# Linear attention and feed-forward on one core: a searched order of operations for the first token group, zero matmuls for TensorE's clock, and the first key chunk on ScalarE's DMA queue

## The chip, the cores and the metric

The kernel runs on one core of one Trainium2 chip. The metric is device time in microseconds (us), the median over executions. Engines are named as in the profile: PE is TensorE's matmuls, PEld its weight loads, DVE is VectorE, ACT is ScalarE, POOL is GpSimd, SP is SyncE, which issues 134 of the 135 DMAs in the kernel before.

## The reference, cut to what matters

```python
q, k, v: (4, 8, 768, 64) float32      # batch, heads, sequence, head width
w_in: (512, 2048), w_out: (2048, 512)

for b in range(12):                   # blocks of 64 positions; the kernel uses 128
    intra = einsum('bhic,bhjc->bhij', qb, kb) * Dmask      # lam ** (i-j), causal
    intra = einsum('bhij,bhjd->bhid', intra, vb)
    inter = einsum('bhid,bhde->bhie', qb * lam_pow, kv_state)
    out[:, :, sl] = intra + inter
    kv_state = lam_block * kv_state + einsum('bhsd,bhse->bhde', kb_dec, vb)
x = out.transpose(0, 2, 1, 3).reshape(3072, 512)
h = x @ w_in
return (h * sigmoid(h)) @ w_out
```

## The kernel before

The 3072 tokens are 24 chunks of 128, and eight token groups of 256 to 512 tokens. For each chunk the kernel scales queries and keys by powers of lam ("pq", "pk"), transposes them on TensorE ("tq", "tk"), copies the transposes to SBUF ("qt", "kt"), computes scores ("s"), masks them ("m"), forms the output ("o") and the running state ("d", "kv"). A group then goes through the up-projection (16 blocks of hidden features, m=0 to 15, through w_in) and the down-projection (through w_out). Weights arrive as float32 and are cast to bf16 on chip ("w"): w_in in five chunks (0 and 1 are the two halves of the rows for m=0..3; chunk 2 is for m=4..7, chunk 3 for m=8..11, chunk 4 for m=12..15), w_out in four.

The order of the first group stands in a string; each word is one operation with its chunk. Every engine's instructions are written in that order, and the trace keeps it: TensorE's work for tq:0, tk:0, d:0, s:0,0, tk:1 and s:0,1 starts at 8.46, 9.46, 9.85, 10.57, 10.97 and 11.40 us.

```python
ORDER = """
pq:0,1 pq:0,0 pk:0 tq:0 vc:0 qt:0 tk:0 d:0 pk:1 qt:1 kt:0,0 kt:0,1 s:0,0 kv:0 tk:1 m:0,0 s:0,1 pq:2,1
... (two lines cut)
vc:3 f:0 w:1 o:3 x:2 xa:3 xb:3 d:3 f:1 kv:3 g:0
"""
    def prep_q1(c, r):                       # half of a pair of query chunks, on GpSimd
        ...
        nc.gpsimd.tensor_tensor(qpairs[c][:, r, :, :], rawq[c][:, :, r, :],
                                lam_fwd[:, NB + c % NB + r, :][:, :, None].to_broadcast([128, H, D]), op=AL.mult)
    # loads, all on SyncE's queue, in this order:
    load_q(0), load_k(0), load_v(0), load_k(1), load_q(2), load_v(1)
    load_k(2), load_k(3), load_v(2), load_v(3)
    for i in range(4):
        load_w("in", i)
    load_q(4)                                # queries of chunks 4 and 5
    load_k(4), load_v(4)
    load_w("in", 4)
    load_k(5), load_v(5)
    load_w("out", 0)
    # after ORDER: m=0..3 of group 0 are done
    cast_w("in", 2)
    ...
    for m in range(4, 8): ffn1(0, m)
    for m in range(8, 11): ffn1(0, m)
    vcast(4)
    tq4 = pe_tq(4, "att", 3); copy_qt(4, tq4), copy_qt(5, tq4)
    tk4 = pe_tk(4, "att", 3)
    copy_kt(4, tk4, 0, nc.vector), copy_kt(4, tk4, 1, nc.vector)
    cast_w("in", 4)                          # on VectorE
    ffn1(0, 11)
    ...
    st_s(4), st_d(4)                         # scores and masks of chunk 4, its state
    ffn1(0, 12)                              # first use of w_in chunk 4
    st_o(4)
    ...
    cast_w("out", 0)
```

## Time and profile before

| | before |
|---|---|
| median of 3 runs | 226.31 us (225.83 to 226.37) |
| profiled run | 226.1 us, span 224.4 us |
| first matmul | 8.46 us |
| m=4 of group 0 starts | 25.94 us |
| w_in chunk 4 has landed | 33.59 us |

All times below are counted from the start of the span. First the page of the kernel before, busy tenths of 40 slices of 5.6 us each, for TensorE, its granted clock and the DMA engines:

```profile
PE   0488998899999999999999999999999999999993
...
PEclk9999999999999999999999999999999999999999
DMA  4999999999959999999999998897420110110212
```

Only the first eight slices of TensorE (45 us) are partly below 9; after them it is full to the end. The DMA row is at 9 in nearly every slice from the second to the 27th: the 16 DMA engines are busy nearly all of that time. The clock row must be read with care. It shows 9 from the start, but the first clock record of this trace, full clock, is at 17.3 us, and until then matmuls issue only every 107 ns (below). What the clock was before that has to be read from the matmuls.

The chain of waits that ended last, by engine:

```profile
PE 82%; DVE 7%; ACT 4%; issue 2%; DMA 2%; POOL 1%
```

Then lines of TensorE's timeline (start, duration, engine, line, output<-inputs, shapes, count; in brackets the idle time before it and what ended it):

```profile
8.46 1.03 PE L271 MATMUL tq<-ident,qb_180 128*128 128x128 bf16 x8 [8.46 <-POOL qb_180 L219]
...
16.83 0.62 PE L285 MATMUL tk<-ident,kb 128*128 128x128 bf16 x4
17.25 0.42 PE L315 MATMUL kv_ps<-vpad_103,kb 128*128 128x128 bf16 x4
...
23.32 8.83 PE L383 MATMUL h_ps<-xt,w_in_bf 128*128 128x256 bf16 x51
...
35.27 0.81 PE L383 MATMUL h_ps<-xt,w_in_bf 128*128 128x512 bf16 x3 [0.60 <-DVE w_in_bf L165]
...
40.39 1.19 PE L398 MATMUL o_ps<-w_out_bf,g 128*128 128x512 bf16 x4 [0.32 <-DVE w_out_bf L167]
```

The first matmul waits for GpSimd's scaled queries. Four matmuls of 128 columns show 0.62 us in one line and 0.42 us in the next: near 17.3 us, where the record of full clock begins, they became almost twice as fast. From the starts of such groups that is one matmul per 107 ns before and 56 ns after. At 35.27 us TensorE waits for VectorE's cast of w_in chunk 4, at 40.39 us for that of w_out chunk 0.

The same stretch on VectorE:

```profile
26.91 1.23 DVE L165 CAST w_in_bf<-w_tmp 128x2048 bf16<-128x2048 f32 x1 [1.64 <-DMA w_tmp<-in_moe_w_in_dram]
...
33.76 1.23 DVE L165 CAST w_in_bf<-w_tmp 128x2048 bf16<-128x2048 f32 x1
35.02 1.29 DVE L341 TENSOR_TENSOR ss<-sp,mask 128x512 bf16<-128x512 f32 x2
```

The cast at 26.91 us (w_in chunk 3) waited 1.64 us for its DMA. The cast at 33.76 us (chunk 4) shows no wait, but the chunk had landed only at 33.59 us, 0.17 us earlier: it had no slack either. The masks of chunk 4 stand behind that cast. Who TensorE waited for between 20 and 45 us (total, times, longest):

```profile
PE h_ps L383 <- DVE w_in_bf L165: 0.6, 1, 0.6
PE o_ps L398 <- DVE w_out_bf L167: 0.3, 1, 0.3
```

### The profile page before, as it was taken

The numbers are of one execution on the slowest core, as the hardware profiler recorded it, in microseconds if no ns is written. First come the engines' busy times: TensorE is split into PE (matmuls) and PEld (weight loads), VectorE is DVE, ScalarE is ACT, GpSimd is POOL, SyncE is SP. The second block draws the span as 40 slices with busy tenths as digits, with TensorE's granted clock in tenths as the row PEclk, the third lists the DMA queues.
The fourth block names the chain that finished last, engine by engine and source line by source line (L and its number), as shares of the span: only waits on it lengthen the run. The fifth ranks groups of instructions, "written<-read, shape, count | busy, mean of one in ns | idle before, by whom it ended". The sixth has DMA issues, their size and how long they took to land.

```text
span 224.4 us, 3867 instructions
## 1 busy us (share of the span) xinstructions
PE 206.6 (92%) x1496; PEld 126.5 (56%) x1520; DVE 93.7 (42%) x181; ACT 100.6 (45%) x199; POOL 51.5 (23%) x58
## 2 busy tenths in 40 slices
PE   0488998899999999999999999999999999999993
PEld 0376755566455786666556656655666644444441
DVE  6468516742168772353443613551454310011121
ACT  4858676444202576455345345444545344433000
POOL 2770051025513222423333330333000000000000
PEclk9999999999999999999999999999999999999999
DMA  4999999999959999999999998897420110110212
GB/s 124 241 223 383 312 269 338 376 235 233 262 148 211 162 217 164 212 203 148 225 211 179 188 248 112 167 203 165 122 67 3 47 50 0 48 47 0 96 47 93
DMA packets 97027, 38.02 MB, mean 169 GB/s; under 512 B 86768, under 2 KB 89840, under 8 KB 97008
## 3 DMA queue, kind: packets, MB, share of 16 engines
q1 hardware_dynamic: 96864, 37.76, 77.8%
q8 instruction: 12, 0.20, 0.4%
q14 instruction: 7, 0.06, 0.1%
q10 hardware_dynamic: 144, 0.00, 0.0%
HBM read 27.27 MB, written 6.29 MB: 150 GB/s over the span
## 4 chain that ended last, share of the span: by engine, by line
PE 82%; DVE 7%; ACT 4%; issue 2%; DMA 2%; POOL 1%
PE h_ps L383 35%; PE o_ps L398 35%; PE op L362 6%; PE sp L336 4%; DVE ss L341 3%; DMA lam_sb<-in_lam_dram 2%; PE kv_ps L315 1%; PE tq L271 1%; DVE ob L402 1%; POOL qb_180 L219 1%; ACT L121 1%; DVE ktbd_104 L262 1%; DVE w_in_bf L165 1%; ACT qt L277 0%; PE tk L285 0%
## 5 line engine op out<-in xcount | busy, mean ns | idle before, releaser
L383 PE MATMUL h_ps<-xt,w_in_bf 128*128 128x384 bf16 (+2 forms) x524 | 98.0, 321 | 1.1 <-DVE w_in_bf L165 0.6
L387 ACT ACTIVATE g<-h_ps 128x384 bf16<-128x384 f32 (+2 forms) x128 | 62.5, 491 | 74.7 <-PE h_ps L383 72.5
L398 PE MATMUL o_ps<-w_out_bf,g 128*128 128x512 bf16 x364 | 91.8, 379 | 1.4 <-DVE w_out_bf L167 0.3
L383 PEld LDWEIGHTS <-w_in_bf 128*128 128x128 bf16 x528 | 50.0, 98 | 33.8 <-DVE w_in_bf L165 0.6
L398 PEld LDWEIGHTS <-g 128*128 128x128 bf16 x384 | 36.7, 98 | 35.7 <-issue 0.7
L402 DVE COPY ob<-o_ps 128x512 f32<-128x512 f32 x24 | 16.6, 692 | 70.4 <-PE o_ps L398 70.3
L230 POOL TENSOR_TENSOR qb<-qf,lam_fwd 128x512 bf16<-128x512 f32 x18 | 18.9, 1053 | 78.8 <-DMA qf<-in_q_dram 78.8
L341 DVE TENSOR_TENSOR ss<-sp,mask 128x512 bf16<-128x512 f32 x48 | 31.0, 685 | 12.9 <-PE sp L336 12.6
L224 POOL TENSOR_TENSOR kb<-kf,lam_bwd 128x512 bf16<-128x512 f32 x24 | 25.2, 1049 | 7.6 <-DMA kf<-in_k_dram 5.8
L369 ACT ACTIVATE xt<-op 128x512 bf16<-128x512 f32 x20 | 11.9, 597 | 23.4 <-PE op L362 23.3
L271 PE MATMUL tq<-ident,qb_180 128*128 128x128 bf16 x8 | 1.0, 310 | 8.5 <-POOL qb_180 L219 8.5
L315 PEld LDWEIGHTS <-kb 128*128 128x128 bf16 x80 | 6.2, 101 | 2.5 <-issue 0.4
L262 DVE CAST kvbd_102<-kv_ps 64x256 bf16<-64x256 f32 x10 | 4.2, 421 | 4.6 <-PE kv_ps L315 4.5
L262 DVE CAST kvbd_108<-kv_ps 64x256 bf16<-64x256 f32 x10 | 4.2, 421 | 3.7 <-PE kv_ps L315 3.5
L271 PEld LDWEIGHTS <-qb_180 128*128 128x128 bf16 x8 | 0.8, 140 | 8.5 <-POOL qb_180 L219 8.5
L336 PE MATMUL sp<-qt,ktbd_104 128*128 128x128 bf16 x48 | 4.1, 235 | 1.0 <-DVE ktbd_104 L262 1.0
L165 DVE CAST w_in_bf<-w_tmp 128x2048 bf16<-128x2048 f32 (+1 forms) x4 | 4.3, 1087 | 1.7 <-DMA w_tmp<-in_moe_w_in_dram 1.6
L219 POOL TENSOR_TENSOR qb_437<-qf_166,lam_fwd 128x512 bf16<-128x512 f32 x2 | 2.0, 1042 | 12.7 <-PE h_ps L383 12.7
L362 PE MATMUL op<-ss,vpad_103 128*128 128x128 bf16 x48 | 4.4, 234 | 0.4 <-DVE ss L341 0.4
L336 PEld LDWEIGHTS <-ktbd_104 128*128 128x128 bf16 x48 | 3.4, 105 | 2.3 <-DVE ktbd_104 L262 1.2
L336 PE MATMUL sp<-qt,ktbd_101 128*128 128x128 bf16 x48 | 4.3, 234 | 0.2 <-ACT qt L277 0.2
L277 ACT ACTIVATE qt<-tq 128x512 bf16<-128x512 bf16 x6 | 3.2, 594 | 2.8 <-PE tq L271 2.8
(98 smaller groups left out, 143.6 us busy)
## 6 DMA issues: line engine op xcount, KB each, us to landing
kf<-in_k_dram SPq DMA_DIRECT2D x24, 256.0 KB, 5.0
vf<-in_v_dram SPq DMA_DIRECT2D x24, 256.0 KB, 5.1
out_dram<-ob SPq DMA_DIRECT2D x24, 256.0 KB, 2.4
qf<-in_q_dram SPq DMA_DIRECT2D x18, 256.0 KB, 3.9
w_tmp<-in_moe_w_out_dram SPq DMA_DIRECT2D x4, 1024.0 KB, 10.1
w_tmp<-in_moe_w_in_dram SPq DMA_DIRECT2D x3, 1024.0 KB, 7.6
w_tmp<-in_moe_w_in_dram SPq DMA_DIRECT2D x2, 512.0 KB, 5.3
qf_138<-in_q_dram SPq DMA_DIRECT2D x1, 512.0 KB, 5.4
```

What stands on the lines that cost most here:

```text
L224: nc.gpsimd.tensor_tensor(kb, rawk.pop(c).rearrange("s (p j) d -> s p j d", j=2), decay(lam_bwd, c % NB), op=AL.mult)
L230: nc.gpsimd.tensor_tensor(qb, rawq.pop(c).rearrange("s (p j) d -> s p j d", j=2), decay(lam_fwd, c % NB), op=AL.mult)
L262: nc.vector.tensor_copy(dst(sl, j), src(sl, j))
L315: nc.tensor.matmul(kv[:, p, :], lhsT=kb[:, p, :, :], rhs=vb[:, p, 0:4:3, :], start=(blk == 0 and p == 0), stop=True, skip_group_check=True)
L336: nc.tensor.matmul(sp[:, p, :], lhsT=kt[:, p, j, :], rhs=qt[:, p, :], start=True, stop=True)
L341: nc.vector.tensor_tensor(ss, sp, mask[:, None, :].to_broadcast([128, 4, BLK]), op=AL.mult)
L362: nc.tensor.matmul(op[:, p, :], lhsT=lhsT, rhs=rhs, start=(i == 0), stop=(i >= len(terms) - NP), skip_group_check=True)
L369: nc.scalar.activation(xt[g][:, :, off * BLK:(off + 1) * BLK], op, AF.Copy)
L383: nc.tensor.matmul(hp[:, a:z], lhsT=w_in_bf[:, ko, m * 128:(m + 1) * 128], rhs=xt[g][:, ko, a:z], start=(ko == 0 and a == 0), stop=(ko == ...
L387: nc.scalar.activation(gg, hp[:, :n], AF.Silu)
L398: nc.tensor.matmul(o, lhsT=gt[g, ko][:, mt * BLK:(mt + 1) * BLK], rhs=w_out_bf[:, ko, :], start=(ko == 0), stop=(ko == KO_OUT - 1))
L402: nc.vector.tensor_copy(ob, o)
```

## The change

The intent: keep the clock up from the start with matmuls on a zero tile ("z"), spread the short operations of the first group over the engines in an order found by search (each word now names its engine, D, A or P, or its PSUM buffer), and bring the first keys in beside the first queries.

```diff
 ORDER = """
-pq:0,1 pq:0,0 pk:0 tq:0 vc:0 qt:0 tk:0 d:0 pk:1 qt:1 kt:0,0 kt:0,1 s:0,0 kv:0 tk:1 m:0,0 s:0,1 pq:2,1
+z:14 pq:0,1,P pq:0,0,D tq:0,h pk:0,D pk:1,P tk:0,o z:2 kt:0,1,D qt:0,A kt:0,0,D qt:1,A s:0,1,o tk:1,h m:0,1,D pq:2,0,D
+s:0,0,att z:2 pq:2,1,P kt:1,0,A s:1,0,o tq:2,att kt:1,1,A pk:2,P m:0,0,D qt:2,A s:1,1,h vc:0,A tk:2,att z:2 m:1,0,D
 ... (rest cut; it ends with the casts of w_in chunk 2 in halves)
+    kf0 = io.tile([128, H, D], F32, name="kf", tag="kf", bufs=6)
+    nc.scalar.dma_start(out=kf0, in_=k[0, :, 0:BLK, :].rearrange("h s d -> s h d"))
+    nc.vector.memset(kvbd[NKV - 1], 0.0)       # first of all: the zero tile
+    nc.gpsimd.memset(ktbd[2], 0.0)             # three memsets go to GpSimd
 ...
-    load_q(0), load_k(0), load_v(0), load_k(1), load_q(2), load_v(1)
-    load_k(2), load_k(3), load_v(2), load_v(3)
+    load_q(0), load_k(1), load_q(2), load_k(2), load_v(0), load_k(3), load_v(1), load_v(2), load_v(3)
 ...
+    def op_z(n, tag="kv"):
+        wt = psum.tile([128, 512], F32, name="warm_ps", tag=tag, bufs=NBUF[tag])
+        zero = kvbd[NKV - 1]
+        for i in range(n):
+            nc.tensor.matmul(wt, lhsT=zero[:, 0, :], rhs=zero.rearrange("d p e -> d (p e)"), start=True, stop=True)
```

Everything after the first group's order is unchanged but for casts of w_in in two halves.

More of the change, by code (lines that the diff above doesn't have):

```diff
@@ L21 @@
 ORDER = """
-pq:0,1 pq:0,0 pk:0 tq:0 vc:0 qt:0 tk:0 d:0 pk:1 qt:1 kt:0,0 kt:0,1 s:0,0 kv:0 tk:1 m:0,0 s:0,1 pq:2,1
-kt:1,1 kt:1,0 m:0,1 s:1,0 pq:2,0 s:1,1 vc:1 m:1,0 o:0 m:1,1 tq:2 pk:2 x:0 o:1 qt:2 tk:2 pk:3 qt:3 x:1 d:1
-kt:2,1 kt:2,0 kv:1 tk:3 s:2,1 kt:3,0 s:2,0 vc:2 m:2,1 s:3,0 kt:3,1 d:2 m:2,0 s:3,1 kv:2 m:3,0 o:2 w:0 m:3,1
-vc:3 f:0 w:1 o:3 x:2 xa:3 xb:3 d:3 f:1 kv:3 g:0
+z:14 pq:0,1,P pq:0,0,D tq:0,h pk:0,D pk:1,P tk:0,o z:2 kt:0,1,D qt:0,A kt:0,0,D qt:1,A s:0,1,o tk:1,h m:0,1,D pq:2,0,D
+s:0,0,att z:2 pq:2,1,P kt:1,0,A s:1,0,o tq:2,att kt:1,1,A pk:2,P m:0,0,D qt:2,A s:1,1,h vc:0,A tk:2,att z:2 m:1,0,D
+m:1,1,D d:0 qt:3,A pk:3,P kt:2,1,D s:2,1,h kt:2,0,D kv:0,A o:0,att s:2,0,h m:2,1,D tk:3,o m:2,0,D vc:1,A d:1
+x:0,A kt:3,0,D kv:1,A s:3,0,att o:1,att kt:3,1,D s:3,1,h vc:2,D m:3,0,D vc:3,D x:1,A m:3,1,D w:0,1,D d:2 kv:2,A
+o:2,att x:2,D w:1,1,D w:1,0,D d:3 o:3,att w:0,0,A f:0,0 x:3,A f:1,0 kv:3,A f:0,1 f:1,1 w:2,0,D w:2,1,D
 """
@@ L97 @@
         kvbd.append(const.tile([128, NP, BLK], BF16, name=f"kvbd{i}"))
-    def clear(i):
+    nc.vector.memset(kvbd[NKV - 1], 0.0)
+    nc.gpsimd.memset(ktbd[2], 0.0)
+    nc.gpsimd.memset(vpad[3], 0.0)
+    nc.gpsimd.memset(ktbd[3], 0.0)
+    for i in range(2):
         nc.vector.memset(vpad[i], 0.0)
@@ L107 @@
     nc.vector.tensor_copy(iota_f, iota_i)
-    clear(0)
-    clear(1)
     lam_exp = const.tile([128, 2 * NB, H], F32)
@@ L116 @@
     )
-    clear(2)
-    clear(3)
+    nc.vector.memset(vpad[2], 0.0)
+    nc.vector.memset(kvbd[2], 0.0)
     lam_fwd = const.tile([128, 2 * NB, H], F32)
@@ L151, in load_w, with move, cast_w @@
         wtmp[which, i] = t
-    def cast_w(which, i):
-        t = wtmp.pop((which, i))
+    def move(e, dst, src):
+        if e == "A":
+            nc.scalar.activation(dst, src, AF.Copy)
+        else:
+            nc.vector.tensor_copy(dst, src)
+    def cast_w(which, i, engs="DD", halves=(0, 1)):
+        t = wtmp[which, i]
         if which == "in":
@@ L160, in cast_w @@
             dst = w_out_bf[:, a:z, :]
-        if which == "in" and i == 0:
-            nc.vector.tensor_copy(dst[:, 0:1, :], t[:, 0:1, :])
-            nc.scalar.activation(dst[:, 1:2, :], t[:, 1:2, :], AF.Copy)
-        elif which == "in":
-            nc.vector.tensor_copy(dst, t)
-        else:
-            nc.vector.tensor_copy(dst[:, 0:2, :], t[:, 0:2, :])
-            nc.vector.tensor_copy(dst[:, 2:4, :], t[:, 2:4, :])
+        n = dst.shape[1] // 2
+        for half, e in zip(halves, engs):
+            move(e, dst[:, n * half:n * half + n, :], t[:, n * half:n * half + n, :])
+    NBUF = {"att": 3, "h": 2, "o": 2, "kv": 1}
     natb, tr, st, kvb, kvps = {}, {}, {}, {}, {}
@@ L189, in load_q @@
         rawq[c] = qf
-    rawq, rawk, vraw = {}, {}, {}
+    rawq, rawk, vraw = {}, {0: kf0}, {}
     def load_1(src, c, tag, bufs):
@@ L213, with prep_q1, prep_k @@
     qpairs = {}
-    def prep_q1(c, r):
+    VG = {"D": nc.vector, "P": nc.gpsimd}
+    def prep_q1(c, r, e="P"):
         if c not in qpairs:
             qpairs[c] = nat.tile([128, 2, H, D], BF16, name="qb2", tag="qb2", bufs=2)
-        nc.gpsimd.tensor_tensor(qpairs[c][:, r, :, :], rawq[c][:, :, r, :],
+        VG[e].tensor_tensor(qpairs[c][:, r, :, :], rawq[c][:, :, r, :],
                                 lam_fwd[:, NB + c % NB + r, :][:, :, None].to_broadcast([128, H, D]), op=AL.mult)
-    def prep_k(c):
+    def prep_k(c, e="P"):
         kb = nat.tile([128, NP, 2, D], BF16, tag="kb")
-        nc.gpsimd.tensor_tensor(kb, rawk.pop(c).rearrange("s (p j) d -> s p j d", j=2), decay(lam_bwd, c % NB),
+        VG[e].tensor_tensor(kb, rawk.pop(c).rearrange("s (p j) d -> s p j d", j=2), decay(lam_bwd, c % NB),
                                 op=AL.mult)
@@ L233, in prep, with vcast @@
         natb[c] = (qb,) + natb[c][1:]
-    def vcast(c):
+    def vcast(c, e="A"):
         if c in vraw:
-            nc.scalar.activation(vpad[c % NKV][:, :, 0:4:3, :],
-                                 vraw.pop(c).rearrange("s (p j) d -> s p j d", j=2), AF.Copy)
+            move(e, vpad[c % NKV][:, :, 0:4:3, :], vraw.pop(c).rearrange("s (p j) d -> s p j d", j=2))
     def dma_t(c):
@@ L262, in half_copy, with pe_tq @@
             nc.vector.tensor_copy(dst(sl, j), src(sl, j))
-    def pe_tq(c, tag="o", bufs=2):
+    def pe_tq(c, tag):
         qb = qpairs.pop(c)
-        tp = psum.tile([128, 2, NP, BLK], BF16, name="tq", tag=tag, bufs=bufs)
+        tp = psum.tile([128, 2, NP, BLK], BF16, name="tq", tag=tag, bufs=NBUF[tag])
         for r in range(2):
@@ L272, in pe_tq, with copy_qt, pe_tk @@
         return tp
-    def copy_qt(c, tp):
+    def copy_qt(c, tp, e="A"):
         i = c % 2
         qt = nat.tile([128, NP, BLK], BF16, tag="qt")
-        nc.scalar.activation(qt.rearrange("d p (s r) -> d p s r", r=2),
-                             tp[:, :, :, 64 * i:64 * i + 64].rearrange("d r p s -> d p s r"), AF.Copy)
+        move(e, qt.rearrange("d p (s r) -> d p s r", r=2),
+             tp[:, :, :, 64 * i:64 * i + 64].rearrange("d r p s -> d p s r"))
         tr[c] = (qt, ktbd[c % NKV])
-    def pe_tk(c, tag="h", bufs=2):
+    def pe_tk(c, tag):
         kb = natb[c][1]
-        tp = psum.tile([128, NP, BLK], BF16, name="tk", tag=tag, bufs=bufs, padded_shape=[128, 2 * NP, BLK])
+        tp = psum.tile([128, NP, BLK], BF16, name="tk", tag=tag, bufs=NBUF[tag], padded_shape=[128, 2 * NP, BLK])
         for p in range(NP):
@@ L286, in pe_tk, with copy_kt @@
         return tp
-    def copy_kt(c, tp, j, eng):
-        kt = ktbd[c % NKV]
-        half_copy(eng, lambda sl, j: kt[sl, :, j, :], lambda sl, j: tp[sl, :, :], j)
+    def copy_kt(c, tp, j, e="D"):
+        rows = slice(64 * j, 64 * j + 64)
+        move(e, ktbd[c % NKV][rows, :, j, :], tp[rows, :, :])
     def st_t(c):
@@ L316, in pe_d, with copy_kv @@
                              start=(blk == 0 and p == 0), stop=True, skip_group_check=True)
-    def copy_kv(c):
+    def copy_kv(c, e="D"):
         if c % NB == NB - 1:
@@ L322, in copy_kv @@
         for j in range(2):
-            half_copy(nc.scalar if c < N0 else nc.vector,
-                      lambda sl, j: kvs[sl, :, 64 * j:64 * j + 64], lambda sl, j: kv[sl, :, 64 * j:64 * j + 64], j)
+            rows = slice(64 * j, 64 * j + 64)
+            move(e, kvs[rows, :, rows], kv[rows, :, rows])
         kvb[c + 1] = kvs
@@ L330, in st_d, with pe_s @@
         copy_kv(c)
-    def pe_s(c, j):
+    def pe_s(c, j, tag="att"):
         qt, kt = tr[c]
-        sp = psum.tile([128, NP, BLK], F32, name="sp", tag="att", bufs=3)
+        sp = psum.tile([128, NP, BLK], F32, name="sp", tag=tag, bufs=NBUF[tag])
         for p in range(NP):
@@ L337, in pe_s, with masked @@
         return sp
-    def masked(sp):
+    def masked(sp, e="D"):
         ss = work.tile([128, 4, BLK], BF16, name="ss", tag="ss")
-        nc.vector.tensor_tensor(ss, sp, mask[:, None, :].to_broadcast([128, 4, BLK]), op=AL.mult)
+        VG[e].tensor_tensor(ss, sp, mask[:, None, :].to_broadcast([128, 4, BLK]), op=AL.mult)
         return ss
@@ L346, in st_s, with pe_o @@
         st[c] = [masked(pe_s(c, j)) for j in range(2)]
-    def pe_o(c):
+    def pe_o(c, tag="att"):
         blk = c % NB
@@ L355, in pe_o @@
             xt[g] = xpool.tile([128, KO_IN, GROUPS[g]], BF16, name="xt", tag="xt", padded_shape=[128, KO_IN, 512])
-        op = psum.tile([128, NP, BLK], F32, name="op", tag="att", bufs=3)
+        op = psum.tile([128, NP, BLK], F32, name="op", tag=tag, bufs=NBUF[tag])
         terms = [(kvb[c][:, p, :], qt[:, p, :], p) for p in range(NP)] if blk > 0 else []
@@ L424 @@
     cell = {}
-    def op_tq(c):
-        cell["tq", c] = pe_tq(c)
-    def op_tk(c):
-        cell["tk", c] = pe_tk(c)
-    def op_kt(c, j):
-        copy_kt(c, cell["tk", c], j, nc.scalar if j == KT_ACT else nc.vector)
-    def op_s(c, j):
-        cell["s", c, j] = pe_s(c, j)
-    def op_m(c, j):
-        st.setdefault(c, [None, None])[j] = masked(cell["s", c, j])
-    def op_o(c):
-        cell["o", c] = pe_o(c)
-    def op_x(c, kos=range(KO_IN), eng=None):
-        op, sl = cell["o", c], slice(kos[0], kos[-1] + 1)
-        dst = xt[0][:, sl, c * BLK:(c + 1) * BLK]
-        if eng is nc.scalar:
-            nc.scalar.activation(dst, op[:, sl, :], AF.Copy)
-        else:
-            nc.vector.tensor_copy(dst, op[:, sl, :])
@@ L452, with keep, run @@
-    table = {
-        "pq": prep_q1, "tq": op_tq, "qt": lambda c: copy_qt(c, cell["tq", c - c % 2]), "pk": prep_k,
-        "tk": op_tk, "kt": op_kt, "vc": vcast, "s": op_s, "m": op_m, "d": pe_d, "kv": copy_kv, "o": op_o,
-        "x": op_x, "xa": lambda c: op_x(c, range(0, 2), nc.scalar), "xb": lambda c: op_x(c, range(2, 4)),
-        "w": lambda i: cast_w("in", i),
-        "f": lambda i: [ffn1(0, m, 0, tag="h" if m < 2 else "o", kos=range(2 * i, 2 * i + 2)) for m in range(4)],
-        "g": lambda i: [ffn1(0, m, 1) for m in range(4)],
+    def keep(name, fn):
+        def run(*args):
+            n = 2 if name == "s" else 1
+            cell[(name,) + args[:n]] = fn(*args)
+        return run
@@ new lines, in op_m, with op_f @@
+    def op_m(c, j, e):
+        st.setdefault(c, [None, None])[j] = masked(cell["s", c, j], e)
+    def op_f(part, half):
+        for m in range(4):
+            ffn1(0, m, part, tag="h" if m < 2 else "o", kos=range(2 * half, 2 * half + 2))
+    def op_z(n, tag="kv"):
[3 more added lines that the diff above has]
+            nc.tensor.matmul(wt, lhsT=zero[:, 0, :], rhs=zero.rearrange("d p e -> d (p e)"), start=True, stop=True)
@@ L459 @@
+    table = {
+        "pq": prep_q1, "tq": keep("tq", pe_tq), "qt": lambda c, e: copy_qt(c, cell["tq", c - c % 2], e),
+        "pk": prep_k, "tk": keep("tk", pe_tk), "kt": lambda c, j, e: copy_kt(c, cell["tk", c], j, e), "vc": vcast,
+        "s": keep("s", pe_s), "m": op_m, "d": pe_d, "kv": copy_kv, "o": keep("o", pe_o),
+        "x": lambda c, e: move(e, xt[0][:, :, c * BLK:(c + 1) * BLK], cell["o", c]),
+        "w": lambda i, h, e: cast_w("in", i, e, (h,)), "f": op_f, "z": op_z,
     }
-    KT_ACT = 1
@@ L461 @@
     for word in ORDER.split():
         name, _, args = word.partition(":")
-        table[name](*[int(a) for a in args.split(",")])
-    cast_w("in", 2)
+        table[name](*[int(a) if a.isdigit() else a for a in args.split(",")])
     load_w("out", 1)
@@ L473 @@
     vcast(4)
-    tq4 = pe_tq(4, "att", 3)
+    tq4 = pe_tq(4, "att")
     copy_qt(4, tq4), copy_qt(5, tq4)
-    tk4 = pe_tk(4, "att", 3)
-    copy_kt(4, tk4, 0, nc.vector), copy_kt(4, tk4, 1, nc.vector)
+    tk4 = pe_tk(4, "att")
+    copy_kt(4, tk4, 0), copy_kt(4, tk4, 1)
     cast_w("in", 4)
@@ L487 @@
     vcast(5)
-    tk5 = pe_tk(5, "att", 3)
-    copy_kt(5, tk5, 0, nc.vector), copy_kt(5, tk5, 1, nc.vector)
+    tk5 = pe_tk(5, "att")
+    copy_kt(5, tk5, 0), copy_kt(5, tk5, 1)
     cast_w("out", 0)
```

## The prediction

> **What bounds it now.** The page: PE busy 206.6 of 224.4 us; the chain of waits: PE 82%. After 45 us PE has hardly a gap, and the change doesn't touch that. The room is in the head. The timeline of PE shows no matmul before 8.46 us (released by POOL's scaled queries), then 17 us of short attention pieces: 128x128 matmuls issue every ~107 ns until 17.3 us, every ~55 ns afterwards, though the page's clock row says 9 from the start. [...] Group 0's up-projection starts m=4 at 25.9 us; PE stands still again until 35.27 us for w_in chunk 4 (0.60 us).
>
> The DMA row is at 9 nearly throughout from 3 to 157 us. Landings in the trace: first queries 6.2, first keys 7.4, w_in chunk 2 22.9, chunk 3 26.9, queries of chunk 4 28.7, its keys 29.8, w_in chunk 4 33.6, w_out chunk 0 38.6 us.
>
> **What the change does.**
> - 14 zero matmuls first (14 x 0.43 us cold, estimate) and six later hold the clock up: some 75 matmuls save about 50 ns each, near 4 us of PE time, much of it hidden behind copies.
> - VectorE takes half of the first query scaling and the first key scaling (0.69 us each, the duration of the mask multiply of that shape, for 1.04 us on POOL); memsets fall into idle time.
> - The first keys share the DMA engines with the first queries. [...] queries land later (about 7.1 us), keys about the same. The first transpose starts at 8.0 to 8.4 us: little gain there.
> - Copies reordered, w_in casts halved.
>
> **Critical path.** I walked the new order with the durations and landings of the trace before (an estimate). m=0..3 end near 23 us and m=4 starts at 23.7 us, paced by w_in chunk 2's landing: about 2 us earlier. Then it is given back. Queries and keys of chunk 4 land at 28.7 and 29.8 us and POOL needs 3 us, so their transposes move 0.5 us at most; w_in chunk 4 lands at 33.6 us, VectorE's cast of it started at 33.76 us, and the masks of chunk 4 queue behind that cast. At the output of chunk 4 (36 us) about 0.2 us are left. More survives only if landings move: the DMA ramps up slowly from 2.5 to 4.5 us, and a second queue may fill some of it (I allow 0.3 to 0.8 us).
>
> **Predicted:** 225.5 us, range 224.2 to 226.6 (before 226.31). Faster by over 2%: 0.03; within 2%: 0.96; slower: 0.01.
>
> **Signs.** Right: 107 ns matmuls end near 5 us; m=4 starts 1.5 to 2.5 us earlier; new PE idle between 23 and 35 us released by w_in casts and POOL's chunk 4; w_in chunk 4 lands within 0.7 us of 33.6; from 45 us on the same blocks, shifted by under 1 us. Wrong: that chunk lands over 1 us earlier, and the head's gain arrives whole.
>
> **What would make it wrong.** The stretch with little DMA traffic at 28.5 to 30 us (80 GB/s) vanishing, which would free up to 1.2 us; an instruction fetch holding up one DMA engine at another time (before: 22.6 us; w_in chunk 3 landed on its last engine 2 us after the first), delaying the first weights; queries landing after 7.5 us.

The sum came to 0.8 us (226.31 to 225.5): about 0.2 us left of the head's gain, and the allowance of 0.3 to 0.8 us for the second queue. The 107 and 55 ns are measured in the kernel before; that zeros bring the clock up early is shown by the kernel after (first record of full clock at 5.6 us instead of 17.3 us). The 7.1 us for the queries and the allowance for the second queue were estimates; no run stood behind them. The ramp of the DMA is measured: 73 GB/s from 2.5 to 3 us, 324 GB/s from 4 to 4.5 us in the trace of the kernel before.

## The result, and the profile after

| | before | after |
|---|---|---|
| median | 226.34 us (225.83 to 226.77, 4 runs) | 226.34 us (226.14 to 226.64, 4 runs) |
| ratio | | 1.0002, 95% interval 0.9978 to 1.0026 |
| first matmul on real data | 8.46 us | 7.30 us |
| first up-projection | 21.10 us | 20.57 us |
| m=4 of group 0 starts | 25.94 us | 25.38 us |
| w_in chunk 4 has landed | 33.59 us | 34.06 us |
| group 1 starts | 43.40 us | 43.98 us |

A ratio is the mean time of one kernel's runs over that of the other's runs of the same rounds, so not quite the ratio of the medians quoted. Executions over 1.5% slower than the fastest of the same kernel are left out of the means.

The time is the same. The page after:

```profile
PE   7779898899999999999999999999999999999993
...
PEclk9999999999999999999999999999999999999999
DMA  4999999999959999999999999499420110110212
```

TensorE is busy from the first slice, but with zeros. The fourth slice has gained a tenth (8 to 9), the fifth (22 to 28 us) has lost one (9 to 8). The chain of waits has changed its nature (by engine, then by line; SPq is SyncE waiting to issue a DMA):

```profile
PE 74%; SPq 13%; DVE 5%; DMA 4%; issue 2%; ACT 0%; DVEq 0%
PE o_ps L408 35%; PE h_ps L393 30%; SPq L205 9%; PE op L372 5%; DMA w_tmp<-in_moe_w_out_dram 4%; PE sp L346 3%; DVE ss L351 2%; SPq L156 2%; SPq L196 2%; PE kv_ps L325 1%; DVE ob L412 1%; DVE kvbd_113 L163 0%; DVE kvbd_110 L163 0%; DVE ktbd_109 L272 0%; DVE w_out_bf L163 0%
```

17% of the span, its first 40 us, now leads back through SyncE's issues and a DMA of w_out: the way to the end goes through the loads. TensorE's timeline:

```profile
1.26 5.33 PE L453 MATMUL warm_ps<-kvbd_113 128*128 128x512 bf16 x14 [1.26 <-DVE kvbd_113 L103]
7.30 0.40 PE L281 MATMUL tq<-ident,qb_195 128*128 128x128 bf16 x4 [0.71 <-DVE qb_195 L230]
8.20 0.40 PE L281 MATMUL tq<-ident,qb_195 128*128 128x128 bf16 x4 [0.50 <-POOL qb_195 L230]
...
20.57 1.92 PE L393 MATMUL h_ps<-xt,w_in_bf 128*128 128x256 bf16 x16 [0.17 <-ACT w_in_bf L161]
22.74 1.92 PE L393 MATMUL h_ps<-xt,w_in_bf 128*128 128x256 bf16 x16 [0.24 <-DVE w_in_bf L163]
25.38 6.39 PE L393 MATMUL h_ps<-xt,w_in_bf 128*128 128x512 bf16 x28 [0.72 <-DVE w_in_bf L163]
...
34.83 1.21 PE L393 MATMUL h_ps<-xt,w_in_bf 128*128 128x512 bf16 x4 [0.44 <-DVE w_in_bf L163]
...
40.97 1.19 PE L408 MATMUL o_ps<-w_out_bf,g 128*128 128x512 bf16 x4 [0.53 <-DVE w_out_bf L163]
```

The zeros take 5.33 us, and the first record of full clock is at 5.6 us. The first transposes start at 7.30 us, 1.16 us earlier than before. The first up-projection is 0.53 us earlier, and m=4 0.56 us (25.38 us). The waits in brackets say where time goes: TensorE now stands before 20.57, 22.74 and 25.38 us for casts of w_in, 1.13 us in all. m=0..3 had ended at 24.66 us. The cast engines, in turn, wait for DMAs; VectorE:

```profile
24.63 1.30 DVE L163 CAST w_in_bf<-w_tmp 128x1024 bf16<-128x1024 f32 x2 [1.95 <-DMA w_tmp<-in_moe_w_in_dram]
27.36 1.30 DVE L163 CAST w_in_bf<-w_tmp 128x1024 bf16<-128x1024 f32 x2 [1.44 <-DMA w_tmp<-in_moe_w_in_dram]
...
34.08 1.30 DVE L163 CAST w_in_bf<-w_tmp 128x1024 bf16<-128x1024 f32 x2 [0.37 <-DMA w_tmp<-in_moe_w_in_dram]
35.41 1.29 DVE L351 TENSOR_TENSOR ss<-sp,mask 128x512 bf16<-128x512 f32 x2
```

Both halves of a cast are merged into one line here. The cast of chunk 2 (24.63 us) waited 1.95 us for its DMA, that of chunk 3 1.44 us, and that of chunk 4 (34.08 us) started as the chunk landed. The masks (35.41 us) are 0.39 us later than before. TensorE's waits between 20 and 45 us:

```profile
PE h_ps L393 <- DVE w_in_bf L163: 1.4, 3, 0.7
PE o_ps L408 <- DVE w_out_bf L163: 0.5, 1, 0.5
```

They were 0.6 and 0.3 us before.

The landings, read from the DMA records of the two traces as the moment when the last of the 16 DMA engines reported:

| landed, us | before | after |
|---|---|---|
| first queries | 6.21 | 6.46 |
| first keys | 7.39 | 7.83 |
| last values of group 0 | 17.35 | 17.63 |
| w_in chunk 0 | 18.85 | 19.87 |
| w_in chunk 1 | 20.21 | 21.89 |
| w_in chunk 2 | 22.92 | 24.61 |
| w_in chunk 4 | 33.59 | 34.06 |
| w_out chunk 0 | 38.60 | 40.20 |
| 16 KB instruction fetches start | 22.6, 39.1 | 19.3, 35.3 |

Two things happened to them. Every landing in the table is later, by 0.25 to 0.47 us for queries, keys, values and w_in chunk 4. And w_in chunks 0 to 2 and w_out chunk 0 are another 0.7 to 1.4 us late. For chunks 1 and 2 and w_out chunk 0 the last row fits that: the trace shows a transfer of 16,384 bytes on a queue that it calls "instruction" (hence the name here), a single packet of 0.98 to 1.31 us in the four of the table, and the data DMA in flight then lands late on its last engine. In the kernel before w_in chunk 3 was the first one hit: first engine 24.81 us, last 26.88 us, a spread of 2.08 us against 0.8 us for the chunks before it. After, it is chunk 1, with 2.20 us. The second fetch starts ahead of the landing of w_out chunk 0 in the kernel after (35.3 against 40.20 us) and behind it in the kernel before (39.1 against 38.60 us): the spread of that chunk is 1.82 and 0.56 us. For chunk 0 it doesn't fit: in two kernels of the experiments below (e1 and e10) chunk 0 also landed late, at 19.89 and 19.64 us with spreads of 1.63 and 1.49 us, although the first fetch came only at 21.5 and 21.0 us. What delays chunk 0 stays open. TensorE's weight loads and matmuls are 3,040 before and 3,080 after, and both traces have 12 of these transfers; which engine's instructions they bring isn't shown. The first came 3.3 us earlier: some 2 us of that go with the 20 zero matmuls and their weight loads (e1, without them, had it at 21.5 us), and the rest comes without any more TensorE instructions.

### The profile page after: what moved, and what is told of

Its sections match the earlier page's. It is cut to its first block, busy times and chain, and to the rows that moved or that the text cites. A ratio compares the mean times of both kernels' runs of the same rounds, so it can differ in the third digit from the quotient of the medians.

```text
span 224.7 us, 3932 instructions
## 1 busy us (share of the span) xinstructions
PE 212.6 (95%) x1540; PEld 125.4 (56%) x1540; DVE 96.5 (43%) x186; ACT 99.4 (44%) x197; POOL 51.9 (23%) x58
## 4 chain that ended last, share of the span: by engine, by line
PE 74%; SPq 13%; DVE 5%; DMA 4%; issue 2%; ACT 0%; DVEq 0%
PE o_ps L408 35%; PE h_ps L393 30%; SPq L205 9%; PE op L372 5%; DMA w_tmp<-in_moe_w_out_dram 4%; PE sp L346 3%; DVE ss L351 2%; SPq L156 2%; SPq L196 2%; PE kv_ps L325 1%; DVE ob L412 1%; DVE kvbd_113 L163 0%; DVE kvbd_110 L163 0%; DVE ktbd_109 L272 0%; DVE w_out_bf L163 0%
## 5 line engine op out<-in xcount | busy, mean ns | idle before, releaser
L408 PE MATMUL o_ps<-w_out_bf,g 128*128 128x512 bf16 x384 | 95.1, 379 | 0.5 <-DVE w_out_bf L163 0.5
L235 POOL TENSOR_TENSOR kb<-kf,lam_bwd 128x512 bf16<-128x512 f32 x23 | 24.3, 1059 | 11.3 <-DMA kf<-in_k_dram 8.5
L453 PE MATMUL warm_ps<-kvbd_113 128*128 128x512 bf16 x20 | 7.1, 508 | 1.3 <-DVE kvbd_113 L103 1.3
L163 DVE CAST w_in_bf<-w_tmp 128x1024 bf16<-128x1024 f32 (+1 forms) x9 | 5.1, 602 | 5.2 <-DMA w_tmp<-in_moe_w_in_dram 5.2
L163 DVE CAST w_out_bf<-w_tmp 128x1024 bf16<-128x1024 f32 x8 | 5.2, 691 | 3.2 <-DMA w_tmp<-in_moe_w_out_dram 3.1
L272 DVE COPY ktbd_106<-kn 64x512 bf16<-64x512 bf16 x8 | 3.7, 463 | 3.1 <-DMA kn<-kb 3.0
L453 PEld LDWEIGHTS <-kvbd_113 128*128 128x128 bf16 x20 | 2.3, 125 | 4.3 <-issue 2.8
L346 PE MATMUL sp<-qt,ktbd_112 128*128 128x128 bf16 x48 | 4.0, 220 | 0.5 <-DVE ktbd_112 L163 0.4
L272 DVE COPY ktbd_103<-kn 64x512 bf16<-64x512 bf16 x8 | 3.1, 385 | 2.9 <-DMA kn<-kb 2.8
```

The lines of the kernel that those rows point to most:

```text
L163: nc.vector.tensor_copy(dst, src)
L235: VG[e].tensor_tensor(kb, rawk.pop(c).rearrange("s (p j) d -> s p j d", j=2), decay(lam_bwd, c % NB), op=AL.mult)
L346: nc.tensor.matmul(sp[:, p, :], lhsT=kt[:, p, j, :], rhs=qt[:, p, :], start=True, stop=True)
L408: nc.tensor.matmul(o, lhsT=gt[g, ko][:, mt * BLK:(mt + 1) * BLK], rhs=w_out_bf[:, ko, :], start=(ko == 0), stop=(ko == KO_OUT - 1))
```

## The experiments

Theory A: landings pace TensorE from about 22 to 42 us, so a faster head only makes it wait. Rival B: the head's gain is lost elsewhere, or isn't there. Further theories are named where they come up. Each ratio is to runs of the kernel before in the same rounds on the same chip; e1 to e4 shared a chip and its runs of before, so did e5 to e8, and e9 to e11. "Cut" kernels load only half of each w_in chunk and cast both halves from it. Their outputs are wrong, which doesn't matter for the times.

| run | median us (range) | ratio to before (95%) | m=4 us | w_in 4 us |
|---|---|---|---|---|
| e1_no_zeros | 226.12 (225.93 to 226.94) | 0.9987 (0.9966 to 1.0009) | 25.15 | 33.89 |
| e2_first_keys_on_sync | 226.25 (225.73 to 226.95) | 0.9991 (0.9968 to 1.0013) | 25.02 | 33.68 |
| e3_before_half_w_in | 225.43 (224.36 to 226.71) | 0.9952 (0.9919 to 0.9985) | 24.23 | 29.16 |
| e4_after_half_w_in | 224.46 (223.97 to 225.33) | 0.9914 (0.9888 to 0.9941) | 23.91 | 29.43 |
| e5_after_half_no_zeros | 225.65 (225.03 to 231.12) | 0.9965 (0.9942 to 0.9987) | slow run | slow run |
| e6_before_half_zeros | 225.33 (223.88 to 226.47) | 0.9944 (0.9906 to 0.9981) | 25.22 | 28.60 |
| e7_loads_and_order_of_chunk_4 | 225.33 (225.12 to 226.15) | 0.9961 (0.9939 to 0.9983) | 24.98 | 31.51 |
| e8_w_in_4_later | 230.14 (228.35 to 230.70) | 1.0153 (1.0115 to 1.0191) | 25.30 | 36.68 |
| e9_before_half_zeros_held | 224.59 (224.03 to 224.99) | 0.9923 (0.9904 to 0.9942) | 24.44 | 28.73 |
| e10_e7_no_zeros | 225.53 (225.20 to 225.98) | 0.9967 (0.9948 to 0.9985) | 25.16 | 31.69 |
| e11_old_head_new_chunk_4 | 226.39 (225.07 to 227.01) | 1.0008 (0.9986 to 1.0031) | 24.72 | 31.29 |
| e12_old_head_zeros_new_chunk_4 | 226.47 (226.00 to 227.59) | 1.0008 (0.9983 to 1.0033) | 26.26 | 32.46 |

The last two columns are of the one profiled execution. For e3 and e11 that was the fastest of its six, so they show the kernel at its best; for e2 and e12 it was the second slowest.

The traces settle one form of rival B, a loss later in the kernel. In each fast trace with complete records (the one of before lacks 24 matmuls), the last 400 matmuls of the up-projection, and all that goes with them to the end, take 171.0 to 171.6 us, while they begin anywhere from 51.4 to 57.0 us. Most of what differs is decided before that.

### e1_no_zeros

```diff
-z:14 pq:0,1,P ... tk:0,o z:2 kt:0,1,D ...
+pq:0,1,P ... tk:0,o kt:0,1,D ...            # every z word out
```

> The kernel after without its 20 zero matmuls, everything else kept. Theory A (the landings of w_in chunk 4 and its neighbours pace TensorE from 25 us on, so the clock in the head is worth nothing in the end): the head runs at 107 ns per 128-column matmul until about 14 to 17 us, m=0..3 of group 0 end up to 1 us later than in the kernel after (24.7 us), but w_in chunk 4 lands within 0.5 us of 34 us and the total is 226.0 to 226.6 us. Rival B (the warm clock really earns time and something else in the change loses as much): 227.3 us or more. A smaller prediction of A: with 40 TensorE instructions fewer, the 16 KB instruction fetches come later again, near 22 and 39 us instead of 19.3 and 35.3 us.

226.12 us: as theory A had it, and the 20 zeros are worth nothing in this kernel that the runs can show. The clock rose at 16.3 us in the profiled run, the first up-projection came at 21.11 us (20.57 with zeros), m=0..3 ended at 24.76 us (24.66 with zeros), and yet m=4 started at 25.15 us (25.38 with zeros), because chunk 2 of w_in landed at 24.38 instead of 24.61 us. The fetches came at 21.5 and 39.7 us.

### e2_first_keys_on_sync

```diff
-    nc.scalar.dma_start(out=kf0, in_=k[0, :, 0:BLK, :]...)
-    load_q(0), load_k(1), load_q(2), ...
+    load_q(0), load_k(0), load_k(1), load_q(2), ...
```

> The kernel after with the first key chunk loaded through SyncE's queue, behind the first queries as in the kernel before. All landings in the kernel after came 0.2 to 0.5 us later than before. Theory C (the second queue delays the landings): they return to those of the kernel before (queries 6.2, keys 7.4, w_in chunk 4 33.6 us) and the time falls to about 225.9 us. Rival (the queue has no part in it; the instruction fetch or chance shifts the landings): w_in chunk 4 stays at 34.0 us and the time at 226.3 us, within 0.2.

The landings did return: queries 6.19, keys 7.39, w_in chunk 4 33.68 us. So in these traces the second queue makes the loads 0.27 to 0.44 us later. The other runs agree: the first queries landed at 6.36 to 6.53 us in the five traces with the second queue and at 6.17 to 6.22 us in eight of the nine without it (6.93 us in e12). The time did not follow clearly: 226.25 us, and the interval holds both 225.9 and 226.3 us. In the trace the second fetch (35.1 us) precedes w_out chunk 0, which landed at 39.97 us, and TensorE waited 0.66 us for it. What the queue alone is worth in time stays open; it is less than these runs can tell apart.

### e3_before_half_w_in and e4_after_half_w_in

```diff
             src = w_in_r[:, k0:k1, a:z]
+            n = (k1 - k0) // 2
+            t, src = t[:, 0:n, :], w_in_r[:, k0:k0 + n, a:z]     # and both casts read t[:, 0:n]
```

> Wrong result on purpose: the kernel before with only half of each w_in chunk loaded and both halves cast from it, so 2 MB less is moved before 34 us and w_in chunk 4 lands about 5 us earlier. Theory A: TensorE loses its waits for w_in and w_out in 34 to 42 us, about 1 us: 225.0 to 225.6 us. m=4 of group 0 starts within 0.4 us of 25.9 us, since the head of the kernel before is not paced by w_in.

> Wrong result on purpose: the same cut of the w_in transfers in the kernel after. Theory A: with the landings out of the way the head's gain arrives: m=4 starts at 23.5 to 24.7 us and the time is 1.2 to 2.2 us below that of the kernel before with the same cut, so 223.0 to 224.2 us. Rival B (the head's gain is lost elsewhere than at landings, or isn't there): the two kernels with the cut stay within 0.5 us of each other.

With 2 MB less to load up to the landing of w_in chunk 4, the two kernels seem to come apart: ratios 0.9952 and 0.9914, or 0.97 us between the medians, where the uncut ones were equal. The two intervals overlap, so this pair alone doesn't prove it. The waits for w_in are gone from e4; for 20 to 45 us the view of waits lists only these:

```profile
PE op L373 <- DVE ss L352: 0.4, 2, 0.2
PE o_ps L409 <- DVE w_out_bf L164: 0.3, 1, 0.3
PE sp L347 <- ACT qt L162: 0.2, 1, 0.2
```

So a gain of the head seems to exist, and what hides it in the uncut kernels is the landing of weights; e5, next, makes that firmer. The size was below the 1.2 to 2.2 us expected, and e4's 224.46 us is outside the forecast. So is m=4 in e3: 24.23 us, where 25.5 to 26.3 us was expected. e3 can be fast by itself: its six times run from 224.36 to 226.71 us, and in the profiled one, the fastest, the clock rose at 12.0 us, not at 17.3 us as in the kernel before, and m=4 was only 0.32 us behind e4's. The same eight matmuls, in the kernel before and in e3:

```profile
13.01 1.03 PE L336 MATMUL sp<-qt,ktbd_104 128*128 128x128 bf16 x8 [0.98 <-DVE ktbd_104 L262]
12.98 0.62 PE L339 MATMUL sp<-qt,ktbd 128*128 128x128 bf16 x8 [0.98 <-DVE ktbd L265]
```

Before and e3 run the same operations until the first weights, and yet their clocks rose 5.3 us apart, at 17.3 and 12.0 us. What sets the moment isn't shown. In the other kernels without zeros the clock rose at 12.0 (e11), 13.0 (e10), 14.2 (e5, to 0.949) and 16.3 us (e1). No kernel was traced twice, so how much one kernel's own moment varies isn't shown.

### e5_after_half_no_zeros and e6_before_half_zeros

e5 is e4 without z words. e6 is e3 with 14 zero matmuls ahead of the first transpose, and the zero tile cleared first:

```diff
+    wt = psum.tile([128, 512], F32, name="warm_ps", tag="kv", bufs=1)
+    for i in range(14):
+        nc.tensor.matmul(wt, lhsT=kvbd[NKV - 1][:, 0, :], rhs=..., start=True, stop=True)
```

> Wrong result on purpose: the kernel after with half the w_in transfers and without its zero matmuls. Theory D (the zeros are worth something only once the landings no longer pace the head): the median is 0.4 to 1.2 us above that of the same kernel with zeros (224.46 us), so 224.9 to 225.6 us, and the single times spread wider[...]. Rival (the zeros are worth nothing even then, the reordering made all of the 1 us between the two cut kernels): within 0.3 us of 224.46 us.

> Wrong result on purpose: the kernel before with half the w_in transfers, with 14 zero matmuls put ahead of its first transpose and nothing else of the change. In the profile of the cut kernel before, the clock rose at 12.0 us and the time was 224.36 us; its other runs went up to 226.71 us. Theory D: with zeros the clock is up at the first transpose in every run, the spread of 2.3 us falls below 1.5 us and the median to 223.9 to 224.6 us, level with the cut kernel after: the zeros are then the whole gain. Rival (the searched order makes the gain): it stays near 225.4 us.

e5: without zeros the cut kernel after loses 0.5% (0.9965 against 0.9914; two chips, each against its own runs of before), so once the landings are out of the way the zeros are worth about 1.2 us, clear of noise. In the uncut kernel they were worth nothing (e1): this contrast is the best evidence that the landings hide what the zeros gain. The times did not spread wider. One of its runs, the profiled one, was slow (231.12 us at a granted clock of 0.952, with a single record of 0.949 from 14.2 us to the end); it is left out of ratio and argument. e6 was a miss: 225.33 us and a spread of 2.6 us, as without zeros. Its trace shows the clock falling back; TensorE's timeline:

```profile
1.25 5.36 PE L469 MATMUL warm_ps<-kvbd 128*128 128x512 bf16 x14 [1.25 <-DVE kvbd L99]
8.42 0.62 PE L277 MATMUL tq<-ident,qb 128*128 128x128 bf16 x8 [1.81 <-POOL qb L225]
...
14.57 1.06 PE L277 MATMUL tq<-ident,qb 128*128 128x128 bf16 x8
```

The same eight transposes take 0.62 us at 8.42 us and 1.06 us at 14.57 us. The clock records say the same: full from 5.7 to 9.1 us, half for 6.8 us until 15.9 us, full again. Between 5.7 and 9.1 us TensorE was busy for about 1.6 us: the zeros ended at 6.6 us, and it then stood for 1.81 us. The mean granted clock of each run counts records alone: the 6.8 us at half clock in a span of 223.5 us make up the 0.985 of this run, while the profiled run of the kernel before has 1.0 in spite of its 17.3 us without a record. It sorts the six times: 0.985 in four runs of 225.21 to 226.47 us, 0.992 in the one of 224.11, 1.0 in the one of 223.88 us. In this kernel fourteen zeros warm the clock; they don't keep it.

### e9_before_half_zeros_held

```diff
-    for i in range(14):                     # e6
+    for i in range(20):
...
+        if word in ("tk:0", "s:0,0", "s:0,1"):
+            zeros(2, "o")
```

> Wrong result on purpose: the kernel before with half the w_in transfers and zero matmuls in the head, now 20 at the start, up to the first transpose, and six more between the first transposes and scores, so that TensorE has no window of low activity after the clock rises. In e6 the clock rose at 5.7 us and fell again from 9.1 to 15.9 us; its runs with a mean granted clock of 0.985 took 225.2 to 226.5 us, those with 0.992 and 1.0 took 224.11 and 223.88 us. Theory D' (a clock that stays up is the whole difference between the two cut kernels): all runs have a granted clock of 0.99 or more and take 223.8 to 224.7 us, ratio to before about 0.991, as for the cut kernel after (0.9914). Rival (the searched order matters too): 0.994 or more although the clock stays up.

From 7 to 20 us TensorE's longest idle time is 0.67 us here, against 1.81 us in e6. The clock was kept up: all six runs have a mean of 0.998 or more, the spread is 0.96 us, the median 224.59 us and the ratio 0.9923. That is level with the cut kernel after (0.9914) within the intervals. So with the old order the held clock is enough to reach it. Against e3 and e6 the intervals overlap, so the size of the step from them is not settled. Whether the searched order adds anything there is not to be told from these runs: e5, the new order without zeros (0.9965), and e3, the old one (0.9952), can't be told apart.

### e8_w_in_4_later

```diff
-    load_w("in", 4)
     load_k(5), load_v(5)
+    load_w("in", 4)
```

> The kernel after with the keys and values of chunk 5 loaded ahead of w_in chunk 4, which then lands about 2.3 us later (near 36.3 us); correct result. Theory A: TensorE waits for it at m=12 and the time rises by nearly that, 1.5 to 2.4 us, to 227.8 to 228.7 us. Rival B (w_in chunk 4 is not what the head waits for): within 0.5 us of 226.3 us.

Chunk 4 landed at 36.68 us, 2.62 us later than in the kernel after, and the time is 1.5% above that of before (230.14 against 226.29 us in the medians), where 227.8 to 228.7 us was expected. TensorE:

```profile
33.97 0.39 PE L325 MATMUL kv_ps<-vpad,kb 128*128 128x128 bf16 x4
37.45 1.89 PE L393 MATMUL h_ps<-xt,w_in_bf 128*128 128x512 bf16 x4 [3.10 <-DVE w_in_bf L163]
39.13 0.63 PE L372 MATMUL op<-qt,kvbd 128*128 128x128 bf16 x4
```

It waits 3.10 us for the cast, and then four matmuls of 512 columns take 1.89 us, where the four before the wait, at 32.60 us, took 1.03 us: the records show half clock from 37.1 to 40.5 us. In this trace, then, the clock fell some 2.8 us into the wait. The single run without such a record (mean clock 1.0) took 228.35 us; the three with 0.993 took 229.94 to 230.70 us. So w_in chunk 4 is what TensorE waits for, and a wait of this length seems to be paid again in clock: the three runs took 1.6 to 2.4 us more than the fourth. This is the one experiment that changes the order of loads and nothing else.

### e7_loads_and_order_of_chunk_4

A version meant to beat both. It loads w_in chunk 4 before the keys and values of chunk 4, and gives TensorE m=12 and m=13 while these arrive.

```diff
     load_q(4)
+    load_w("in", 4)
     load_k(4), load_v(4)
-    load_w("in", 4)
     load_k(5), load_v(5)
...
+    tq4 = pe_tq(4, "att"); copy_qt(4, tq4), copy_qt(5, tq4)
+    cast_w("in", 4)
+    ffn1(0, 11), ffn1(0, 12)
+    prep_k(4)
+    ffn1(0, 13)
+    tk4 = pe_tk(4, "att")
+    copy_kt(4, tk4, 0, "D"), copy_kt(4, tk4, 1, "A")        # shared between VectorE and ScalarE
     ...
+    st_s(5)
+    ffn1(1, 0, 0), ffn1(1, 1, 0)                            # half the columns of group 1, while chunk 5 ends
+    pe_d(5), st_o(5)
+    cast_w("out", 0)
+    ffn2(0, 0, range(0, 4)), ffn2(0, 1, range(0, 4))
```

(First keys on SyncE's queue, as in e2. Shortened.)

> A version meant to beat both, correct result: the kernel after with the first keys on SyncE's queue, w_in chunk 4 loaded ahead of the keys and values of chunk 4, the work on chunks 4 and 5 moved behind the matmuls m=12 to m=15 of group 0, its copies shared with ScalarE, and two up-projections of group 1 begun on half their columns while chunk 5 finishes. If landings pace TensorE, w_in chunk 4 lands near 32 us, the wait for it goes, and the steady part starts 1 to 1.7 us earlier: 224.6 to 225.4 us. If the order of loads doesn't matter: 226.2 us.

It is 0.4% faster than the kernel before (0.9961, interval 0.9939 to 0.9983), correct, 225.33 us. Chunk 4 landed at 31.51 us, and TensorE goes through m=11 to m=13 without a gap:

```profile
22.34 1.92 PE L391 MATMUL h_ps<-xt,w_in_bf 128*128 128x256 bf16 x16 [0.55 <-DVE w_in_bf L161]
24.98 6.39 PE L391 MATMUL h_ps<-xt,w_in_bf 128*128 128x512 bf16 x28 [0.72 <-DVE w_in_bf L161]
...
31.65 2.91 PE L391 MATMUL h_ps<-xt,w_in_bf 128*128 128x512 bf16 x12
```

The two waits for w_in chunks 1 and 2 (0.55 and 0.72 us) remain. Since e7 changes loads, order of work and engines together, it doesn't say which of them gives the 0.4%.

### e10_e7_no_zeros and e11_old_head_new_chunk_4

e10 is e7 without z words. e11 is e7 with the head of the kernel before: its order written with engine letters, its order of loads, no zeros.

> The version e7 without its zero matmuls, correct result. In e7 TensorE still waits for the landings of w_in chunks 1 and 2 (0.55 and 0.72 us before 22.3 and 25.0 us), so by theory A the warm head is hidden behind those even there: within 0.4 us of e7, 225.0 to 225.8 us, ratio 0.995 to 0.998. If the zeros carry e7: 226.0 us or more.

> The head of the kernel before (its order of operations and of loads, no zeros; its casts of w_in halved) with e7's loads and order for chunks 4 and 5, correct result. The old head starts m=4 near 25.9 us where e7 starts it at 25.0 us with the landing of chunk 2 as the limit; with w_in chunk 4 landing at 31.5 us nothing later should take those 0.9 us back. Theory A: 225.7 to 226.3 us, 0.4 to 0.9 us above e7. Rival (the head is hidden here too): 225.1 to 225.5 us, and the whole gain of e7 is the order of chunk 4.

e10 is level with e7 (0.9967 and 0.9961): the zeros are not needed there either. In its profiled run the clock rose at 13.0 us and m=4 started at 25.16 us, 0.18 us after e7's; TensorE had waited 1.15 us for the cast of chunk 2:

```profile
25.16 6.39 PE L391 MATMUL h_ps<-xt,w_in_bf 128*128 128x512 bf16 x28 [1.15 <-DVE w_in_bf L161]
```

e11 is level with the kernel before (1.0008, 226.39 us, just above its forecast), and 0.86 us above e10, which ran beside it. Its best run, the profiled one, took 225.07 us with the clock up at 12.0 us and m=4 at 24.72 us (25.9 us was expected), its worst 227.01 us. Take four kernels: before (old head, old chunk 4: 226.2 to 226.4 us), after (new head, old chunk 4: 226.34 us), e11 (old head, new chunk 4: 226.39 us), e7 and e10 (both new: 225.33 and 225.53 us). Either part alone gives nothing; together they give 0.4%. So the searched order, with its order of loads, seems to earn some 0.7 to 0.9 us once the work on chunk 4 no longer takes it back, and without zeros. That is barely clear of noise: the intervals of e10 and e11 just fail to touch, and the means of all six times each are 0.70 us apart, give or take 0.75 us. The next run asks whether e11's spread comes from the moment of the clock's rise.

### e12_old_head_zeros_new_chunk_4

```diff
-pq:0,1,P pq:0,0,P pk:0,P ...                # e11
+z:20 pq:0,1,P pq:0,0,P pk:0,P ...           # and z:2,o after tk:0, s:0,0 and s:0,1
```

> Kernel e11 (head of the kernel before, e7's loads and order for chunks 4 and 5) with the zero matmuls of e9 added: 20 at the start and six between the first transposes and scores; correct result. e11's times spread from 225.07 us, in the profiled run where the clock rose at 12.0 us, to 227.01 us. If it is the moment of the clock's rise that spreads them, the clock is up before 8 us here, every time is 225.0 to 225.8 us and the ratio to before 0.995 to 0.998, level with e7 and e10. If the spread has another cause, it stays near 2 us and the median near 226.2 us.

A miss: 226.47 us, spread 1.59 us, although the clock was up at 5.6 us in the profiled run. That run took 227.17 us, the second slowest of the six. In it TensorE and VectorE waited for w_in chunk 0:

```profile
19.40 0.61 PE L369 MATMUL op<-ss,vpad 128*128 128x128 bf16 x8
21.58 1.14 PE L390 MATMUL h_ps<-xt,w_in_bf 128*128 128x256 bf16 x8 [1.57 <-DVE w_in_bf L160]
```

```profile
21.10 0.43 DVE L160 CAST w_in_bf<-w_tmp 128x512 bf16<-128x512 f32 x1 [1.52 <-DMA w_tmp<-in_moe_w_in_dram]
```

The chunk landed at 21.07 us against 18.73 us in e11. Some 0.6 us of this is an execution whose loads were late from the start (last values at 17.95 against 17.38 us). The rest goes with the fetch, at 18.0 us instead of 20.8 us: chunk 0's spread over the DMA engines is 2.33 us against 0.61 us. The 26 zeros are 52 instructions, and with them the fetch comes just before the first weights. That this costs what the clock gains is argued, not shown: it is one execution, and not a typical one. The mean clock of the slowest run (227.59 us) was 0.992, the lowest of the six, so the clock may not have held in every run either.

## Why the prediction was right or wrong

The time, 226.34 us, is inside the range of 224.2 to 226.6 us and 0.84 us above the 225.5 us predicted; "within 2%" was right. The range held no change at all as well, so being inside it says little: of a gain of 0.8 us nothing came, and three terms of the sum below were mis-sized. What speaks for the prediction is the mechanism.

- **The mechanism was right**: the head gains and the landings of weights take it back. The zeros are worth nothing in the uncut kernel (e1) and about 1.2 us when the weights land early (e4 against e5); e8 makes one landing later, and the end comes later. The cut pair e3 and e4 and the version e7 point the same way, the first within noise, the second with several changes at once.
- **Clock**: right. Full clock at 5.6 us; and, as the text allowed, "much of it hidden": in e1 all of it was, as far as the runs can show.
- **Scaling of queries and keys**: the first transposes came at 7.30 and 8.20 us, where 8.0 to 8.4 us was predicted. Queries landed at 6.46 us, not 7.1. The term of 1.04 us for GpSimd was mis-sized: its half now runs beside VectorE's and takes 1.54 us:

```profile
6.60 1.54 POOL L230 TENSOR_TENSOR qb_195<-qf_140,lam_fwd 128x512 bf16<-128x512 f32 x1 [1.77 <-ACT lam_bwd L128]
8.93 1.04 POOL L235 TENSOR_TENSOR kb<-kf,lam_bwd 128x512 bf16<-128x512 f32 x1 [0.78 <-DMA kf<-in_k_dram]
```

  VectorE's half had started at 6.55 us and took 0.69 us. For the next pair GpSimd's half started first (10.72 us, 1.04 us), and VectorE's, at 10.78 us, took 1.53 us.

- **"m=4 starts at 23.7 us ... about 2 us earlier"**: this step failed in size. It measured 25.38 us, 0.56 us earlier. The prediction took the landing of w_in chunk 2 as 22.9 us; it was 24.61 us. From there m=4 came 0.77 us later, where 0.8 us was predicted. The instruction fetch, named there as a risk, came at 19.3 instead of 22.6 us. In all eight uncut kernels whose first fetch started before 22 us (18.0 to 21.5 us) chunk 2 landed at 23.95 to 25.15 us; only in the kernel before, with the fetch at 22.6 us, did it land at 22.92 us. No run moved the fetch alone. The landing isn't the whole of it: m=0..3 ended at 24.66 us, not "near 23 us", and 0.41 us of that are waits for chunks 0 and 1.
- **"At the output of chunk 4 (36 us) about 0.2 us are left"**: none were; the masks came 0.39 us later than before (35.41 against 35.02 us), since chunk 4 of w_in landed 0.47 us later.
- **"A second queue may fill some of it (I allow 0.3 to 0.8 us)"**: wrong in sign. The landings came 0.25 to 0.47 us later, and e2 brings them back by undoing only that part. That allowance could be much of the missing 0.84 us; e2's time is too uncertain to prove it.
- **New idle between 23 and 35 us released by w_in casts and GpSimd's chunk 4**: right (0.72, 0.19 and 0.44 us before 25.38, 32.41 and 34.83 us).

Open: what the second queue costs in time, what delays w_in chunk 0, what the searched order gives in the cut kernels, and what spreads the times of e11 and e12.

## What to carry to other kernels

Before speeding up a stretch, write down when the data that its end needs have landed. Here the DMA engines were busy through nearly all of the head (9 tenths or more in all but the first of its eight slices), an earlier start turned into a wait at the next landing, and time came only from the order of loads together with the order of work that needs them (0.4%, without any zero matmul). Warm-up matmuls had to bridge the thin stretches up to the real work here, not only start early: with 14 ahead of it four of six runs had a mean clock of 0.985 (e6), with 20 ahead and six in between all six had 0.998 or more (e9). They are also instructions, and the instruction fetch came earlier with them: at 19.3 us against 21.5 us without (after, e1), at 18.0 against 20.8 us (e12, e11).
